# Block-sorted attention and a squared-ReLU layer: x^T of one head pair by TensorE, key copies by VectorE alone, one more pair of tiles by seven products, and a new order

## The chip, the cores and the metric

The kernel runs on one core of a Trainium2 chip. The metric is the device time of one execution in microseconds. The core has TensorE (PE, matmuls, with its weight loads shown apart as PEld), VectorE (DVE), ScalarE (ACT), GpSimd (POOL), SyncE (SP, which here only issues DMAs), and 16 DMA engines. Each engine works through its own instructions in the order in which the program lists them; engines wait for each other through semaphores. A difference of about 0.2% can be told from none for this kernel.

## The reference

Four batches, eight heads, 768 positions of 64 dimensions. A small matrix per head (8 x 8 blocks) is made nearly doubly stochastic by five rounds of exponential and normalisation; it mixes the blocks of 96 positions of the keys and of the values; each block of queries attends to its own mixed block. The result, as 3072 tokens of 512 values, goes through two matrix products with a squared ReLU between them.

```python
for _ in range(5):
    P = np.exp(P - np.max(P, axis=-1, keepdims=True))
    P = P / (np.sum(P, axis=-1, keepdims=True) + 1e-09)
    P = P / (np.sum(P, axis=-2, keepdims=True) + 1e-09)
k_sorted = np.einsum('bhij,bhjcd->bhicd', P, k_b)      # and v_sorted
attn = softmax(scale * q_b @ k_sb^T);  x = attn @ v_sb  # per block of 96
h = np.maximum(x @ w_in, 0.0)                           # 512 -> 2048
out = h * h @ w_out                                     # 2048 -> 512
```

(The softmax is written short here; in the reference it is spelled out.)

## The kernel before

**Attention.** A unit is one batch b (0 to 3, called batches 1 to 4) and one pair of heads hp (0 to 3), in stages that the program names by letters. For batch 1 and half of batch 2, keys and values are mixed by large matmuls with expanded matrices (K, V, L659 and L695). For the rest, `s_nat` (N for the keys, V for the values; L815) mixes them in their natural layout with 32 x 32 matmuls, evacuates them to `kn` and `vn` (ACT and DVE, one bank each), and the transposition is left to the DMA: `s_turn` (Z) issues a DMA transpose of `kn` into `kx` (k_turn, L870) and one of the queries, `qi` into `qz` (q_turn, L897); k_blocks then copies `kx` (128 x 768) into the tile `kvT`, in the order of positions that the scores want. The values go to a DRAM scratch `v_way` and come back as `vblk` (L839, L845). Then follow the scores (S: L730 on PE, the exponential into `et` on ACT, L759), the product with the values (A: L921, then a reciprocal and a multiplication on DVE, L931 and L932, which write `ao`), and x^T (X, `s_xt`): `ao` is transposed into the tile `xT`, either by a DMA transpose that SP issues (L956) or by TensorE (L974) with a copy out of PSUM by ACT or DVE.

**The layer.** `up_block` multiplies w_in by x^T (L1066), ACT takes the ReLU into `h` (L1074), and ACT or DVE squares it into `hid` (L1081, L1083). `plain_block` multiplies one tile of 128 tokens by w_out: 16 matmuls of 512 columns (L1153) and a copy out. `pair_block` multiplies two tiles of 128 tokens at once by a two-by-two block scheme with seven products instead of eight: sums of `hid` on DVE (L1201, written into a part of `xT` that is free), seven products of 8 matmuls of 256 columns each (L1241, with w_out or the precomputed sums `wsum`), kept parts (copied out by ACT or DVE into `xT`) and joins on DVE (L1272, which add a kept part to a product and write `ob`, 128 x 256). The products are called p1a, p2a, p1b, p2b, p5, p6, p3, p7, p4; p4 goes to the bank that p7's join frees. Batch 1 has two groups of 384 tokens with three plain blocks each, the other batches have groups of 256 tokens with one pair block each, the last one with its end taken apart.

**What sets the order.** The program first lists every operation with a cost and its dependencies, in a planner (`Plan`). DUES gives each attention stage a due time, which sorts the stages and says how much of the layer's matmul work has to pass before a stage may be preferred to it. LEAD says how many pieces of the next up block come ahead of the last block of a group, LAG how many places the last product (p4) is moved back among them. The planner then plays the program through with its costs: an operation that allows ACT or DVE (AD) goes to the one that would end it first. The order in which it starts the operations is the order of the program, for every engine. So a changed cost or due time can move any instruction.

**DMA gates.** The loads of batches 3 and 4 (`kb`, `vb`, `qb`, issued by POOL) are held back by `load_late`: a copy of a few elements of `xT` on POOL (hold) waits for the DMA transposes of x^T of the batch before. A similar copy (gate) early in the program orders one transpose behind a load. The first key of `s_turn`'s DMA transposes waits until all loads of its batch are there.

Of the kernel before, what the change touches and what calls it, by code (L numbers as in the profile page):

```python
# [18 lines left out]


DUES = {
    (0, "K"): (-816.984375, -817.0, -816.96875, -709.984375),
    (0, "S"): (-718.96875, -816.953125, -718.984375, -709.96875),
    (0, "T"): (-760.5, -816.9375, -719.0, -709.953125),
    (0, "A"): (-718.0, -734.5, -718.953125, -623.984375),
    (0, "X"): (-710.0, -624.0, -718.5, -599.0),
    (0, "W"): (-719.0,),
    (1, "V"): (-625.5, -599.0),
    (1, "Q"): (-599.0,),
    (1, "N"): (None, -598.984375),  # L30
    (1, "Z"): (None, None, -598.96875, -598.953125),
    (1, "S"): (-599.0, 33.5, 38.015625, 47.5),
    (1, "A"): (38.0, 36.5, 40.5, 47.5),
    (1, "X"): (47.53125, 40.5, 47.515625, 47.5),
    (2, "L"): (55.0,),
    (2, "N"): (69.515625, 62.5),
    (2, "V"): (69.5, 69.5625),
    (2, "Z"): (69.53125, 69.546875, 69.578125, 83.515625),
    (2, "S"): (69.59375, 89.0, 89.015625, 89.03125),
    (2, "A"): (83.5, 89.0, 89.078125, 89.046875),  # L40
    (2, "X"): (83.53125, 89.0625, 92.515625, 92.5),
    (3, "L"): (125.5,),
    (3, "N"): (125.53125, 125.515625),
    (3, "V"): (125.5, 134.5),
    (3, "Z"): (134.546875, 129.5, 134.515625, 136.015625),
    (3, "S"): (136.0, 134.5, 134.5625, 136.046875),
    (3, "A"): (136.0, 134.53125, 136.0, 136.0625),
    (3, "X"): (171.5, 136.03125, 138.5, 161.5),
}

TURNED = 1
WSUM = 0
LEAD = (0, 0, 2, 8, 0, 2, 12, 0, 12, 14, 1)
LAG = (0, 0, 2, 1, 2, 1, 2, 0, 2, 2, 0)


FIRST = ("K0' v0 K1 v1 S0 t0' S1 t1' A0 K2' V2 A1 K3 S2 t2 v3 S3 x1' A2 T3' x0' A3 X2' F0 F1 F3 "
# [155 lines left out]
def kernel(  # L215
# [213 lines left out]
    def loads_after(deps):  # L429
        for g in range(4):  # L430
            if g == 1:
                landed["last"] = plan.add("DMA", 0.4, lambda e: None, [landed["last"]])
            t = slice(NT // 4 * g, NT // 4 * (g + 1))
            dma(("w_out", g), 1.05, lambda t=t: (w_out_bf[:, t, :], w_out_r[:, t, :]), deps)
        def gate(e):
            nc.gpsimd.tensor_copy(out=xT[0:1, 0:HP - 1, HS:HS + 1],
                                  in_=w_out_bf[0:1, NT // 2 - HP + 1:NT // 2, 0:1])

        for t, g in ((2, 0), (2, 1), (1, 0), (0, 0), (1, 1), (0, 1)):
            if t == 0 and g == 1:  # L440
                holds["gate"] = plan.add("POOL", 0.1, gate, [landed["w_out", 1]])
                deps = [holds["gate"]]
            load(1, t, HP * g, HP, deps=deps)
            if t == 2 and g == 1:
                landed["last"] = plan.add("DMA", 1.5, lambda e: None, [landed["last"]])
# [417 lines left out]
    def s_turn(u):  # L863

        b, hp = u.b, u.hp
        m, op = k_nat[b, hp]
        kx, oldx = rkx.take()

        def k_turn(e):
            nc.sync.dma_start_transpose(  # L870
                out=kx_r[kx].rearrange("p (a x) -> p a x", a=NA),
                in_=kn_r[m].rearrange("p a e d -> p (a e d)"))

        def k_blocks(e):
            copy(e, u.ksT[:, 0:S].rearrange("p (n x) -> p n x", n=NB),
                 kx_r[kx].rearrange("p (x n) -> p n x", n=NB))

        sp = plan.add("SP", 1.4, k_turn, [op, loaded(b)] + oldx)
        k_op = plan.add("WAY", 1.3, lambda e: None, [sp])
        rkn.use(m, k_op)  # L880
        u.k_op = plan.add(AD, (0.8, 0.87), k_blocks, [k_op] + u.old)
        rkx.use(kx, k_op, u.k_op)

        n, oldi = rqi.take()

        def q_pair(e):
            nc.vector.tensor_copy(
                out=qi_r[n].rearrange("p a e d -> p e a d"),
                in_=qkv[b][0][:, 2 * hp:2 * hp + 2, :].rearrange("p e (a d) -> p e a d", d=D))

        qp = plan.add("DVE", 0.4, q_pair, [landed[b, 0, HP * (2 * hp // HP), 0]] + oldi)
        readers[b].append(qp)
        rqi.use(n, qp)
        u.qz, oldz = rqz.take()

        def q_turn(e):
            nc.sync.dma_start_transpose(  # L897
                out=q_late(u.qz), in_=qi_r[n].rearrange("p a e d -> p (a e d)"))

        sp = plan.add("SP", 1.4, q_turn, [qp, loaded(b)] + oldz + [op for ops in rvs.all for op in ops])  # L900
        u.q_op = plan.add("WAY", 1.3, lambda e: None, [sp])
        rqi.use(n, u.q_op)
        rqz.use(u.qz, u.q_op)

    def s_av(u, due=0):
        nao, olda = rao.take()
        if u.b > 0:
            w, u.vs_op = v_blk[u.b, u.hp // 2]
        u.norms = []
        for hf in u.halves:  # L910
            st = {}

            slot, old = r2.take()

            def mm(e, hf=hf, st=st, slot=slot):
                if hf == u.halves[0]:
                    u.ao = att.tile([96, u.ni, 2, D], BF16, tag="ao", name="ao", bufs=3)
                st["p"] = oup = p2[slot]
                for n in range(NQ):
                    for h in range(2):  # L920
                        nc.tensor.matmul(  # L921
                            out=oup[:, h, 66 * n:66 * n + D + 1],
                            lhsT=et_r[u.et[hf]][:, h, BLK * n:BLK * n + 128],
                            rhs=(u.vs[:, NQ * hf + n, h, 0:D + 1] if u.b < 1 else
                                 vb_r[w][:, NQ * hf + n, 2 * (u.hp % 2) + h, 0:D + 1]),
                            start=True, stop=True)

            def norm(e, st=st, n0=NQ * hf - u.i0):
                ov = st["p"][0:96, :, 0:66 * NQ].rearrange("p e (n x) -> p e n x", x=66)
                rec = att.tile([96, 2, NQ], FP32, tag="rec", name="rec")  # L930
                nc.vector.reciprocal(out=rec, in_=ov[:, :, :, D])  # L931
                nc.vector.tensor_tensor(  # L932
                    out=u.ao[:, n0:n0 + NQ, :, :].rearrange("p n e d -> p e n d"),
                    in0=ov[:, :, :, 0:D],
                    in1=rec[:, :, :, None].to_broadcast([96, 2, NQ, D]),
                    op=ALU.mult)

            s2 = slot
            pe = plan.add("PE", 0.26, mm, u.exps[hf] + [u.vs_op] + old
                          + (olda if hf == u.halves[0] else []), due)  # L940
            op = plan.add("DVE", 0.9, norm, [pe])
            r2.use(s2, pe, op)
            ret.use(u.et[hf], pe)
            if u.b < 1:
                rvs.use(u.m, pe)
            else:
                rvb.use(w, pe)
            u.norms.append(op)
        u.nao = nao

    def s_xt(u, due=0, eng=AD, own=True):
        early = u.b == 0 and u.halves == (1,) and u.hp < TURNED
        if early or u.b > 1 or u.b == 1 and u.hp < HP - 1:
            def turn(e):
                t0 = S * u.b + BLK * u.i0
                nc.sync.dma_start_transpose(  # L956
# [96 lines left out]
    def up_block(t0, n, c0, g):  # L1053
# [7 lines left out]
        def one(nts):  # L1061
# [23 lines left out]
            def add(m):  # L1085
# [12 lines left out]
                if m < len(nts) - 1:  # L1098
# [1 line left out]
                w = n * len(nts)  # L1100
                s1, old1 = rh1.take()
                r = plan.add("ACT", cost_f(w)[0], relu, st["pe"] + old1)
                sq = plan.add(AD, cost_b(w), square,
                              [r] + [u for c in chunks for u in h_users[c][-1:]])
                rf.use(st["s"], r)
                rf.pinned.discard(st["s"])
# [232 lines left out]
    def ffn_all():  # L1339
        ups = [up_block(0, HS, 0, 0), up_block(HS, HS, 1, 1)]  # L1340
        pairs = [[plain_block(0, 0) + plain_block(TT, 1) + plain_block(2 * TT, 2)],
                 [plain_block(HS, 1) + plain_block(HS + TT, 2) + plain_block(HS + 2 * TT, 3)]]
        for t0 in range(S, n_tok, 2 * TT):
            g = len(ups)
            c = 2 * (g % 2)
# [3 lines left out]
        for g, up in enumerate(ups):  # L1349
            items += up  # L1350
            after = ups[g + 1] if g + 1 < len(ups) else []
            for n, block in enumerate(pairs[g]):
                if n == len(pairs[g]) - 1:
                    items += after[:LEAD[g]]
                    del after[:LEAD[g]]
                items += block
                if g > 1:
                    moves.append((block[-1], LAG[g] if n == len(pairs[g]) - 1 else 1))
            if g == 0:
                items.append(weight_sums)  # L1360
# [81 lines left out]
    def load_late(b, n, due):  # L1442

        def hold(e):
            nc.gpsimd.tensor_copy(out=held[0:1, 0:HP - (b == 2), b:b + 1],  # L1445
                                  in_=xT[0:1, 0:HP - (b == 2), S * b - 1:S * b])

        holds[b] = plan.add("POOL", 0.1, hold, [x_done[b - 1, x, 0] for x in range(HP - (b == 2))])
        landed["last"] = plan.add("DMA", 4.5, lambda e: None, [holds[b]])
        for g in range(2):  # L1450
            for t in (1, 2, 0):
                load(b, t, HP * g, HP)
# [52 lines left out]
```

## Time and profile before

| | |
|---|---|
| median of 3 runs | 215.31 us (215.30 to 215.32) |
| profiled execution | 215.62 us, of which the span from first to last instruction 213.8 us |
| mean granted TensorE clock | 0.999 of full |
| PE busy | 205.9 us, 2435 matmuls |
| ACT busy | 138.6 us, 272 instructions |
| DVE busy | 136.6 us, 355 instructions |
| POOL busy | 28.2 us |
| DMA | 31.77 MB, mean 149 GB/s |

How to read it: a row of groups names the line, the engine, the operation, what it writes and reads with shapes, and how often; then the busy time in us and the mean in ns of one, and the idle time of the engine ahead of them with what ended it. The chain is the work that ended last, followed back from the end of the program: each piece stands with its start, its length, and its engine and line. A window's row gives its bounds, its length, and the busy time of PE, PEld, DVE, ACT and POOL with the number of instructions, then the clock granted to PE, the DMA engines' share and GB/s. The profile gives matmul ends that are modelled, so a busy PE is not one at its peak.

### The profile page before, as it was taken

What the parts mean: (1) busy time and instruction counts of PE and PEld (TensorE: products, weight loads), DVE (VectorE), ACT (ScalarE), POOL (GpSimd) and SP (SyncE); (2) the same over time, 40 slices, a digit from 0 to 9 for tenths busy, and PEclk for the clock granted to TensorE, in tenths of its full rate; (3) what the DMA queues carried; (4) which work ended last, traced back from release to release, by engine and by line L of the source; (5) the groups of instructions that cost most, each with busy time, mean ns of one, the idle gap of its engine ahead of it and who ended that gap; (6) DMA issues with size and microseconds to landing.
All of it is one profiled execution on the core that took longest, in us unless ns stands there. A gap on an engine that the chain in (4) does not pass through costs nothing.

```text
span 213.8 us, 5958 instructions
## 1 busy us (share of the span) xinstructions
PE 205.9 (96%) x2435; PEld 154.7 (72%) x2435; DVE 136.6 (64%) x355; ACT 138.6 (65%) x272; POOL 28.2 (13%) x54
## 2 busy tenths in 40 slices
PE   8998999999999999999999899999999999999994
PEld 2566765445654588687878688877988788888882
DVE  5877769644584427867966637677869647436442
ACT  4787997339993456579889256388769268538230
POOL 7769221000000700000000420000000000000000
PEclk9999999999999999999999999999999999999999
DMA  6999999999684799299984499759995510020022
GB/s 150 216 202 206 207 207 209 191 231 286 139 187 63 137 213 227 61 186 209 188 141 141 69 179 243 145 163 107 260 158 147 103 67 3 0 101 0 0 101 98
DMA packets 47035, 31.77 MB, mean 149 GB/s; under 512 B 26464, under 2 KB 42080, under 8 KB 47008
## 3 DMA queue, kind: packets, MB, share of 16 engines
q0 software_dynamic: 12224, 13.24, 37.8%
q1 hardware_dynamic: 34784, 18.15, 37.6%
q8 instruction: 19, 0.31, 0.6%
q14 instruction: 8, 0.07, 0.1%
HBM read 29.70 MB, written 8.72 MB: 180 GB/s over the span
## 4 chain that ended last, share of the span: by engine, by line
PE 80%; ACT 10%; DVE 5%; issue 3%; DMA 1%; DVEq 0%; ACTq 0%
PE pf L1066 33%; PE pf L1241 23%; PE pf L1153 9%; PE p L730 3%; PE p L921 3%; ACT h L1074 2%; ACT kvT L284 2%; PE p L815 2%; ACT et L759 2%; ACT hid L1081 1%; DVE xT L1201 1%; PE p L695 1%; DMA p_sb<-in_sort_net_dram 1%; PE p L486 1%; PE vbp L779 1%
## 5 line engine op out<-in xcount | busy, mean ns | idle before, releaser
L1066 PE MATMUL pf<-xT,w_in_bf 128*128 128x256 bf16 (+1 forms) x698 | 89.4, 282 | 0.1
L1066 PEld LDWEIGHTS <-w_in_bf 128*128 128x128 bf16 x698 | 66.1, 98 | 14.6 <-issue 1.4
L1074 ACT ACTIVATE h<-pf 128x512 bf16<-128x512 f32 (+1 forms) x104 | 56.9, 568 | 20.5 <-PE pf L1066 19.4
L1083 DVE TENSOR_TENSOR hid<-h 128x512 bf16<-128x512 bf16 (+1 forms) x82 | 33.1, 405 | 30.4 <-ACT h L1074 29.2
L1241 PEld LDWEIGHTS <-xT 128*128 128x128 bf16 x288 | 27.4, 98 | 5.0 <-DVE xT L1201 1.2
L1241 PE MATMUL pf<-wsum,xT 128*128 128x256 bf16 x216 | 27.1, 273 | 0.1
L1241 PEld LDWEIGHTS <-hid 128*128 128x128 bf16 x216 | 20.6, 98 | 3.5 <-issue 1.1
L932 DVE TENSOR_TENSOR ao<-p,rec 96x512 bf16<-96x512 f32 x32 | 22.0, 687 | 1.1
L1153 PE MATMUL pf<-w_out_bf,hid 128*128 128x512 bf16 x96 | 22.6, 379 | 0.0
L284 ACT COPY xT<-pf 128x256 f32<-128x256 f32 (+1 forms) x28 | 10.6, 377 | 18.2 <-PE pf L1241 12.2
L759 ACT ACTIVATE et<-p 96x384 bf16<-96x384 f32 x48 | 19.7, 492 | 2.4 <-PE p L730 2.4
L284 ACT COPY ob<-pf 128x256 f32<-128x256 f32 (+1 forms) x14 | 6.5, 464 | 19.9 <-PE pf L1153 12.3
L1272 DVE TENSOR_TENSOR ob<-pf,xT 128x256 f32<-128x256 f32 x27 | 11.4, 424 | 11.0 <-PE pf L1241 8.7
L1241 PE MATMUL pf<-w_out_bf,hid 128*128 128x256 bf16 x144 | 18.0, 273 | 0.0
L1153 PEld LDWEIGHTS <-hid 128*128 128x128 bf16 x96 | 8.7, 97 | 9.2 <-issue 0.2
L931 DVE RECIPROCAL rec<-p 96x8 f32<-96x8 f32 x32 | 6.4, 200 | 12.1 <-PE p L921 10.4
L921 PEld LDWEIGHTS <-et 96*128 96x128 bf16 x256 | 11.4, 97 | 3.5 <-issue 0.8
L1201 DVE TENSOR_TENSOR xT<-hid 128x512 bf16<-128x512 bf16 (+1 forms) x27 | 13.0, 510 | 0.6
L1081 ACT ACTIVATE hid<-h 128x512 bf16<-128x512 bf16 (+1 forms) x22 | 12.9, 593 | 0.5
L1445 POOL COPY held<-xT 1x3 bf16<-1x3 bf16 (+1 forms) x2 | 0.4, 186 | 83.1 <-DMA xT<-ao 83.1
L1241 PE MATMUL pf<-w_out_bf,xT 128*128 128x256 bf16 x72 | 9.4, 273 | 0.6 <-DVE xT L1201 0.6
L1241 PE MATMUL pf<-wsum,hid 128*128 128x256 bf16 x72 | 9.3, 272 | 0.6 <-DVE ob L1272 0.5
(103 smaller groups left out, 203.5 us busy)
## 6 DMA issues: line engine op xcount, KB each, us to landing
out_dram<-ob SPq DMA_DIRECT2D x23, 256.0 KB, 2.5
v_way<-vn SPq DMA_DIRECT2D x6, 396.0 KB, 5.7
vblk<-v_way SPq DMA_DIRECT2D x6, 396.0 KB, 4.3
vb<-in_v_dram POOLq DMA_DIRECT2D x6, 384.0 KB, 12.9
kb<-in_k_dram POOLq DMA_DIRECT2D x6, 384.0 KB, 11.6
qb<-in_q_dram POOLq DMA_DIRECT2D x6, 384.0 KB, 14.3
w_in_bf<-in_moe_w_in_dram POOLq DMA_DIRECT2D x4, 512.0 KB, 9.7
w_out_bf<-in_moe_w_out_dram POOLq DMA_DIRECT2D x4, 512.0 KB, 13.9
```

Of the source, the lines that this page charges most:

```text
L284: nc.scalar.copy(out=out, in_=in_)
L759: nc.scalar.activation(out=et[:, h, 0:HS].rearrange("p (n c a) -> p n c a", c=C0, a=NA), in_=st["p"][0:96, h, 0:HS].rearrange("p (n a c) - ...
L921: nc.tensor.matmul(out=oup[:, h, 66 * n:66 * n + D + 1], lhsT=et_r[u.et[hf]][:, h, BLK * n:BLK * n + 128], rhs=(u.vs[:, NQ * hf + n, h, 0: ...
L932: nc.vector.tensor_tensor(out=u.ao[:, n0:n0 + NQ, :, :].rearrange("p n e d -> p e n d"), in0=ov[:, :, :, 0:D], in1=rec[:, :, :, None].to_b ...
L1066: nc.tensor.matmul(out=pf_r[st["s"]][:, n * m:n * (m + 1)], lhsT=w_in_bf[:, kc, 128 * nt:128 * (nt + 1)], rhs=xT[:, kc, t0:t0 + n], start= ...
L1074: nc.scalar.activation(out=st["h1"][:, 0:n * len(nts)], in_=pf_r[st["s"]][:, 0:n * len(nts)], func=AF.Relu)
L1081: nc.scalar.activation(out=dst, in_=h1, func=AF.Square)
L1083: nc.vector.tensor_tensor(out=dst, in0=h1, in1=h1, op=ALU.mult)
L1153: nc.tensor.matmul(out=pf_r[st["s"]], lhsT=hid[:, nt, TT * c:TT * (c + 1)], rhs=w_out_bf[:, nt, :], start=(nt == 0), stop=(nt == NT - 1))
L1201: lambda e: nc.vector.tensor_tensor(out=s_view(n, js), in0=a, in1=bb, op=op), deps + st["old", n])
L1241: nc.tensor.matmul(out=pf_r[st[bank]][:, cols], lhsT=a, rhs=r, start=(first and j == 0), stop=(j == NJ - 1), skip_group_check=n in (3, 4, ...
L1272: op = plan.add("DVE", 0.15 + 1.04e-3 * DH, lambda e: nc.vector.tensor_tensor(out=get()[:, cols], in0=pf_r[st[bank]][:, 0:DH], in1=buf, op ...
```

## The change

- `s_xt`: for batches 3 and 4 (b = 2, 3), the last head pair's x^T (hp = 3) is made by eight TensorE transposes and a copy of 128 x 768 out of PSUM, where it was a DMA transpose. CROSS says for each batch how many head pairs still use the DMA. Batch 4's loads are accordingly held for three transposes, not four, and the early gate reads one column, not three.
- k_blocks may run on DVE alone; before, the planner chose between ACT and DVE.
- Batch 1's second group of 384 tokens: one plain block and one pair block instead of three plain blocks.
- All due times, LEAD and LAG are new, and three costs of the planner (q_pair, norm, the square on ACT), so that the stages and with them the instructions of every engine stand in a new order. LAG now applies to every block that ends with p4.

The first line of CROSS moves all later lines by one: L974 is L975 in the changed kernel, and so on.

```diff
 DUES = {
-    (0, "K"): (-816.984375, -817.0, -816.96875, -709.984375),
+    (0, "K"): (-924.375, -959.328125, -1014.625, -571.03125),
...
-    (3, "X"): (171.5, 136.03125, 138.5, 161.5),
+    (3, "X"): (173.046875, 152.640625, 167.296875, 157.984375),
 }
+CROSS = (0, 3, 3, 3)
 TURNED = 1
 WSUM = 0
-LEAD = (0, 0, 2, 8, 0, 2, 12, 0, 12, 14, 1)
-LAG = (0, 0, 2, 1, 2, 1, 2, 0, 2, 2, 0)
+LEAD = (0, 0, 2, 12, 0, 10, 8, 0, 12, 14, 14)
+LAG = (3, 3, 2, 3, 3, 1, 3, 0, 2, 2, 3)
...
         def gate(e):
-            nc.gpsimd.tensor_copy(out=xT[0:1, 0:HP - 1, HS:HS + 1],
-                                  in_=w_out_bf[0:1, NT // 2 - HP + 1:NT // 2, 0:1])
+            nc.gpsimd.tensor_copy(out=xT[0:1, 0:TURNED, HS:HS + 1],
+                                  in_=w_out_bf[0:1, NT // 2 - TURNED:NT // 2, 0:1])
...
-        u.k_op = plan.add(AD, (0.8, 0.87), k_blocks, [k_op] + u.old)
+        u.k_op = plan.add("DVE", 0.87, k_blocks, [k_op] + u.old)
...
-        qp = plan.add("DVE", 0.4, q_pair, [landed[b, 0, HP * (2 * hp // HP), 0]] + oldi)
+        qp = plan.add("DVE", 0.36, q_pair, [landed[b, 0, HP * (2 * hp // HP), 0]] + oldi)
...
-            op = plan.add("DVE", 0.9, norm, [pe])
+            op = plan.add("DVE", 0.92, norm, [pe])
...
-        if early or u.b > 1 or u.b == 1 and u.hp < HP - 1:
+        if early or u.b > 0 and u.hp < CROSS[u.b]:
...
-                sq = plan.add(AD, cost_b(w), square,
+                sq = plan.add(AD, (cost_b(w)[0] + 0.04, cost_b(w)[1]), square,
...
-                 [plain_block(HS, 1) + plain_block(HS + TT, 2) + plain_block(HS + 2 * TT, 3)]]
+                 [plain_block(HS + 2 * TT, 3), pair_block(HS, HS + TT, 1, 2, 0)]]
...
-                if g > 1:
+                if block[-1].__name__ == "p4":
                     moves.append((block[-1], LAG[g] if n == len(pairs[g]) - 1 else 1))
...
-            nc.gpsimd.tensor_copy(out=held[0:1, 0:HP - (b == 2), b:b + 1],
-                                  in_=xT[0:1, 0:HP - (b == 2), S * b - 1:S * b])
+            nc.gpsimd.tensor_copy(out=held[0:1, 0:CROSS[b - 1], b:b + 1],
+                                  in_=xT[0:1, 0:CROSS[b - 1], S * b - 1:S * b])
 
-        holds[b] = plan.add("POOL", 0.1, hold, [x_done[b - 1, x, 0] for x in range(HP - (b == 2))])
+        holds[b] = plan.add("POOL", 0.1, hold, [x_done[b - 1, x, 0] for x in range(CROSS[b - 1])])
```

How the instructions stand at three places, before and in the change. In the rows, `kvT_92`, `kx_130`, `kn_125`, `qi_126`, `et_131`, `wsum_161`, `vblk_121` and the like are buffers of the tiles named above, `p_0_78`, `p_1_79` and `pf_80` to `pf_82` are PSUM banks, and `xtp` is the PSUM tile of the TensorE transposes.

ACT before, at batch 3's last head pair: two kept parts of a pair block, the key copy for the last scores, and the exponentials of the third and the fourth head pair.

```order
L284 COPY xT<-pf_82 128x256
L284 COPY xT<-pf_81 128x256
L284 COPY kvT_92<-kx_130 128x768
L759 ACTIVATE et_131<-p_0_78 96x384 x2
L759 ACTIVATE et_134<-p_1_79 96x384 x2
L759 ACTIVATE et_137<-p_0_78 96x384 x2
L284 COPY ob<-pf_81 128x256
```

DVE in the change, where the same copy now stands:

```order
L287 COPY kvT_108<-kx_129 128x768
L932 RECIPROCAL rec<-p_0_78 96x8
L933 TENSOR_TENSOR ao<-p_0_78,rec 96x2x4x64
L932 RECIPROCAL rec<-p_1_79 96x8
L933 TENSOR_TENSOR ao<-p_1_79,rec 96x2x4x64
L287 COPY kvT_92<-kx_130 128x768
L1273 TENSOR_TENSOR ob<-pf_81,xT 128x256
L1273 TENSOR_TENSOR ob<-pf_82,xT 128x256
```

The copy left ACT's queue, where exponentials were behind it, for DVE's, where two joins are behind it.

PE before, in the pair block that runs beside the end of batch 4's attention, from p7 (`wsum_161`) to p4 (`wsum_162`):

```order
L1241 MATMUL pf_82<-wsum_161,xT 128x256
L1241 LDWEIGHTS xT
L1241 MATMUL pf_82<-wsum_161,xT 128x256
L1241 LDWEIGHTS hid
L1241 MATMUL pf_82<-wsum_162,hid 128x256
```

And in the change:

```order
L1242 LDWEIGHTS xT
L1242 MATMUL pf_82<-wsum_161,xT 128x256
L975 LDWEIGHTS ao
L975 MATMUL xtp<-ident,ao 128x96
L975 LDWEIGHTS ao
L975 MATMUL xtp<-ident,ao 128x96
L975 LDWEIGHTS ao
```

Eight transposes (the first are shown) now stand between the two products.

SP before, at the end of batch 4's transposes:

```order
L870 DMA_TRANSPOSE kx_130<-kn_125 128x6x128
L897 DMA_TRANSPOSE qz_97<-qi_126 128x6x128
L845 DMA vblk_121<-v_way 96x2112
L956 DMA_TRANSPOSE xT<-ao 128x8x96
L1127 DMA out_dram<-ob 128x512 x2
L956 DMA_TRANSPOSE xT<-ao 128x8x96 x3
```

And in the change:

```order
L871 DMA_TRANSPOSE kx_130<-kn_125 128x6x128
L898 DMA_TRANSPOSE qz_97<-qi_126 128x6x128
L957 DMA_TRANSPOSE xT<-ao 128x8x96
L846 DMA vblk_121<-v_way 96x2112
L1128 DMA out_dram<-ob 128x512 x3
L957 DMA_TRANSPOSE xT<-ao 128x8x96 x2
```

The first x^T transpose moved ahead of the read of the values, and the fourth one is gone.

More of the change, by code (lines that the diff above doesn't have):

```diff
@@ L21 @@
 DUES = {
-    (0, "K"): (-816.984375, -817.0, -816.96875, -709.984375),
[L23 to L45, printed above, removed]
@@ L46 @@
-    (3, "S"): (136.0, 134.5, 134.5625, 136.046875),
-    (3, "A"): (136.0, 134.53125, 136.0, 136.0625),
-    (3, "X"): (171.5, 136.03125, 138.5, 161.5),
+    (0, "K"): (-924.375, -959.328125, -1014.625, -571.03125),
+    (0, "S"): (-915.09375, -924.8125, -910.28125, -482.65625),
+    (0, "T"): (-576.4375, -926.625, -883.203125, -570.125),
+    (0, "A"): (-563.34375, -892.640625, -856.546875, -424.234375),
+    (0, "X"): (-415.0, -878.71875, -417.515625, -421.5),
+    (0, "W"): (-894.859375,),
+    (1, "V"): (-418.078125, -417.4375),
@@ new lines @@
+    (1, "Q"): (-416.0625,),
+    (1, "N"): (None, -415.9375),
+    (1, "Z"): (None, None, 30.03125, 35.0625),
+    (1, "S"): (33.5, 35.9375, 36.0625, 38.03125),
+    (1, "A"): (36.03125, 36.046875, 37.953125, 38.046875),
+    (1, "X"): (38.015625, 40.921875, 40.9375, 42.953125),
+    (2, "L"): (41.5,),
+    (2, "N"): (43.25, 60.203125),
+    (2, "V"): (63.734375, 81.46875),
+    (2, "Z"): (68.296875, 70.84375, 90.734375, 91.03125),
+    (2, "S"): (81.46875, 90.890625, 91.0, 91.140625),
+    (2, "A"): (85.46875, 90.96875, 91.015625, 91.46875),
@@ L49 @@
+    (2, "X"): (90.296875, 100.046875, 91.84375, 97.28125),
+    (3, "L"): (104.28125,),
+    (3, "N"): (115.921875, 112.328125),
+    (3, "V"): (120.859375, 123.515625),
+    (3, "Z"): (135.3125, 123.0, 123.5, 140.5),
+    (3, "S"): (147.0, 123.90625, 145.09375, 154.15625),
+    (3, "A"): (149.28125, 127.078125, 152.609375, 155.5),
+    (3, "X"): (173.046875, 152.640625, 167.296875, 157.984375),
 }
+CROSS = (0, 3, 3, 3)
 TURNED = 1
 WSUM = 0
-LEAD = (0, 0, 2, 8, 0, 2, 12, 0, 12, 14, 1)
-LAG = (0, 0, 2, 1, 2, 1, 2, 0, 2, 2, 0)
+LEAD = (0, 0, 2, 12, 0, 10, 8, 0, 12, 14, 14)
```

## The prediction

> **What bounds the kernel now.** I read the page's busy shares first, then the chain, then the windows at the places where TensorE (PE) stands idle, then the groups by form.
>
> ```profile
> PE 205.9 (96%) x2435; PEld 154.7 (72%) x2435; DVE 136.6 (64%) x355; ACT 138.6 (65%) x272; POOL 28.2 (13%) x54
> ...
> PE 80%; ACT 10%; DVE 5%; issue 3%; DMA 1%; DVEq 0%; ACTq 0%
> ```
>
> PE is busy for 96% and makes up 80% of the chain that ended last. So there are only two ways to gain: fewer matmul microseconds, or less idle time of PE. The next view gives the idle time (window, its length, PE busy, then weight loads, DVE, ACT and POOL).
>
> ```profile
> 12.00:171.00 159.00, 155.53 (x1944) 114.77 (x1945) 107.25 (x238) 109.72 (x214) 19.91 (x38) 1.00 0.91 173
> 18.00:20.00 2.00, 1.50 (x25) 1.21 (x23) 1.81 (x6) 1.33 (x3) 2.00 (x3) 1.00 1.25 210
> 61.00:65.00 4.00, 3.70 (x46) 2.07 (x45) 3.31 (x7) 4.00 (x12) 0.00 (x0) 1.00 0.85 143
> 98.00:99.00 1.00, 0.58 (x11) 0.29 (x10) 0.09 (x1) 1.00 (x2) 0.00 (x0) 1.00 1.65 279
> 119.00:122.00 3.00, 2.30 (x20) 1.55 (x18) 1.77 (x4) 1.12 (x3) 1.68 (x4) 1.00 0.30 47
> 149.00:150.00 1.00, 0.73 (x19) 0.64 (x20) 0.40 (x2) 1.00 (x3) 0.00 (x0) 1.00 0.57 203
> 169.00:171.00 2.00, 1.49 (x15) 1.18 (x13) 0.76 (x2) 0.00 (x0) 0.00 (x0) 1.00 0.72 170
> ```
>
> From 12 to 171 us PE idles 159.00 - 155.53 = 3.47 us, of which 0.50, 0.30, 0.42, 0.70, 0.27 and 0.51 lie in the six short windows, 2.70 together. That pool is about all that a better order can win. What ended the waits is in the chain (start, length, what):
>
> ```profile
> 97.25 1.59 ACT kvT L284
> 98.89 0.51 PE p L730 x16
> ...
> 108.32 1.16 ACT kvT L284
> ...
> 118.20 1.04 DVE xT L1201 x2
> ...
> 147.61 1.61 ACT kvT L284
> 149.27 0.51 PE p L730 x16
> ...
> 169.71 0.43 DVE ob L1272
> 170.19 1.03 PE pf L1241 x8
> ```
>
> At 98.89 and 149.27 the scores (L730) wait for ScalarE's (ACT's) copy of the sorted keys into kvT. At 108.32 such a copy delays the exponentials behind it on ACT, these the squares, these the sums on VectorE (DVE, L1201), and after 119 the products that read the sums pay. At 170.19 p4 waits for the join of p7, which stands right ahead of it.
>
> **The copies into kvT.**
>
> ```profile
> L284 ACT COPY kvT<-kx 128x768 bf16<-128x768 bf16 x5 | 8.0, 1591 | 0.0
> L286 DVE COPY kvT<-kx 128x768 bf16<-128x768 bf16 x5 | 4.2, 850 | 0.0
> ```
>
> ACT takes 1.59 us, DVE 0.85, and of ten such copies each had five. All ten are now DVE's: ACT loses 8.0 us of 138.6, DVE gains 4.2. Engine totals cost or win nothing by themselves (both were at 65%); what counts is where the copy stands. The one of 108.32 stood on ACT right ahead of the exponentials of batch 3's last head pair, and on DVE it now stands between a norm and two joins (first pieces of the order, above). The exponentials no longer have it ahead of them; the joins behind it come later by 0.85, and a matmul block waits for the bank that each frees. I count the windows at 98 (0.42), 119 (0.70) and 149 (0.27) as gone: -1.39. With two of them goes a slow restart, since the scores take 0.51 there and 0.45 in a place without a wait (below): -0.1. If DVE comes late to the copies or the joins, this returns; that is a rival.
>
> **Matmul work.** Batch 1's second half had three plain blocks; two of them become one pair block of seven products.
>
> ```profile
> 50.68 0.45 PE p L730 x16
> ...
> 64.95 0.87 PE pf L1153 x4
> ...
> 74.04 0.34 PE xtp L974 x8
> ...
> 123.37 0.87 PE pf L1066 x8
> ```
>
> Two plain blocks are 32 matmuls of 512 columns, 0.87/4 each: -6.96. The seven products are 56 matmuls of 256 columns, 0.87/8 each (L1066 has the same shape): +6.09. The two x^T blocks of the last head pair add 16 transposes at 0.34/8: +0.68. The sum is -0.19: most of what the seven products save goes into the transposes. The pair block also adds six sums and three joins on DVE and some copies on ACT; the blocks around it are another 7 us of matmuls and more, with no evacuation of a plain block to wait for, so I price them at nothing, and at 0.4 (one join, as at 169.71) if p4 should wait there.
>
> The Trainium skill, "TensorE: Matmul & The Clock Gate", Part 4 (PE-mode transpose), speaks against the transposes: it gives about 275 ns for one of 128x128 bf16 in a kernel's context, so 16 would be an estimated 4.4 us and the change would lose. The row above has eight in 0.34 us, 43 ns apiece; the trace differs, and the sum keeps 0.68.
>
> **x^T of the last head pair.** Before, a DMA transpose followed the last norm; now PE and a copy do it.
>
> ```profile
> L286 DVE COPY xT<-xtp 128x768 bf16<-128x768 bf16 x1 | 0.6, 558 | 1.1 <-PE xtp L974 1.1
> xT<-ao SPq DMA_TRANSPOSE x12, 3.2
> ```
>
> 3.2 us from issue to landing become 0.34 on PE and 0.56 on DVE, so x^T is ready 2.3 us sooner. The up block that reads it did not wait for it at 171 before (p4 ran until then), so this counts only in that it lets the block follow sooner. In batch 4 the transposes stand between p7 and p4 (second pieces). Before, p4's first row came right behind p7's last. The eight transposes, 0.34 us, cover most of the 0.51 that PE idled for p7's join: -0.3.
>
> **The rest of the order.** The windows at 18 (0.50) and 61 (0.30) keep dependencies of the same kind (an exponential or a copy on ACT ahead of an L921); the bounds are all or nothing, I take half: -0.4. The four joins of batch 4's keys and values come closer to each other, with 0.9 us of other matmuls between two of them, while an evacuation takes up to 0.96:
>
> ```profile
> L286 DVE CAST vn<-p 128x768 bf16<-128x768 f32 x6 | 5.7, 956 | 1.8 <-PE p L815 1.7
> L931 DVE RECIPROCAL rec<-p 96x8 f32<-96x8 f32 x32 | 6.4, 200 | 12.1 <-PE p L921 10.4 <-ACT h L1074 1.5
> L932 DVE TENSOR_TENSOR ao<-p,rec 96x512 bf16<-96x512 f32 x32 | 22.0, 687 | 1.1
> ```
>
> Three such gaps could each cost up to 0.2, so 0 to 0.6, and I take +0.3.
>
> **What SP gets to wait for.** Ahead of the last read of batch 4's values (vblk) there now stands an x^T, which waits for ao; before, vblk came first (third pieces). SP's rows of before:
>
> ```profile
> 142.07 1.24 SPq L870 DMA_TRANSPOSE kx<-kn  x1
> 144.74 2.11 SPq L870 DMA_TRANSPOSE kx<-kn  x1
> 148.01 1.92 SPq L897 DMA_TRANSPOSE qz<-qi  x1
> 154.39 1.24 SPq L897 DMA_TRANSPOSE qz<-qi  x1
> 155.72 0.53 SPq L845 DMA_DIRECT2D vblk<-v_way  x1
> 156.35 1.95 SPq L956 DMA_TRANSPOSE xT<-ao  x1
> vblk<-v_way SPq DMA_DIRECT2D x6, 396.0 KB, 4.3
> ```
>
> In the new order 64 matmuls of 0.109 (7.0 us), two score steps (0.9) and two half steps of L921 (0.5) lie between the L921 that feeds this ao and the first that reads vblk: 8.4 us. The way there: two norms of 0.20 + 0.69 (1.8), the issue of the transpose (1.24 to 1.95), that of vblk (0.53) and 4.3 to landing, 7.9 to 8.6 if SP is free. SP's pace: from the first kx at 142.07 to the end of the last qz at 155.63 it took 13.6 us; in the new order 14.4 us of blocks lie between batch 4's first join (L815) and that L921; the first kx goes out 4 us after that join, behind a v_way that waits for the third one's evacuation, and the norms add 1.8, so it has 12.2 us, and by that pace SP is 1.4 us late. But part of the pace was a wait for ACT's copies to free kx, which now take half as long. PE waits 0 to 1.8 us; I take +0.5, and +0.1 at batch 3, where x^T also stands ahead of a vblk. Queued behind on PE is everything, since it works in order.
>
> **The sum**, from the profiled execution (215.62 us: span 213.8 and 1.8 around it; 0.31 above the median of 215.31): -1.39 - 0.1 - 0.19 - 0.3 - 0.4 + 0.3 + 0.5 + 0.1 = -1.48. That is 214.1 for a profiled execution and **213.8 us** for the median. With the open bounds, the likeliest case lies between 212.8 and 214.8.
>
> **Rivals.**
>
> *DVE becomes the bound of the last attention stage.* Copies, joins, sums and norms go through one queue in order:
>
> ```profile
> L1201 DVE TENSOR_TENSOR xT<-hid 128x512 bf16<-128x512 bf16 (+1 forms) x27 | 13.0, 510 | 0.6
> ```
>
> In the new order six norms (5.3 us), four sums (2.0), three joins and a copy of the output (1.7) and one square (0.4) stand in a row, 9.4 us, beside 10.3 us of PE's blocks: hardly any slack, and a norm that waits for its L921 holds all behind it. Against it: the rows overlap a little, and norms before were done in time. Then the 1.5 us come back as waits for ao and joins: 215.3, no change.
>
> *SP's queue makes vblk late by much* (the slower side). The mechanism is that above. If all eight transposes of batch 4 issue at 1.95 us instead of 1.24 (+5.7 us), vblk lands some 4 us after its need instead of 0.5, and batch 3's 1 us late: 213.8 + 3.5 + 0.9 = 218.2 at the most, and 216.2 halfway to it. From 1.5 us more lateness than I took, it outweighs the gain. For it: two of the rows above were at 1.92 and 2.11. Against: the others were at 1.24.
>
> *The gain is not on the path.* Other waits of the same length stand behind those removed, on ACT above all, whose relus and exponentials still set when banks come free. Only the matmul sum is left: 215.1, no change.
>
> *The transposes don't overlap each other.*
>
> ```profile
> L974 PE MATMUL xtp<-ident,ao 96*128 96x96 bf16 x24 | 1.9, 206 | 0.0
> ```
>
> One by one they would take 16 x 0.206 = 3.3 us instead of 0.68: 213.8 + 2.6 = 216.4. By the skill's page above it would be an estimated 217.5. The row of eight in 0.34 us leaves it a chance of 0.01.
>
> **How the numbers follow.** Forecast 0.62, DVE bound 0.14, SP late 0.11, no gain 0.12, transposes 0.01. About 0.2% (0.43 us) is what a measurement of this kernel can tell from no change, so faster is below 214.88. Nearly all of the forecast falls there (0.60), and of the DVE, SP and no-gain cases those parts in which only some waits return (0.11): faster 0.71. Slower: 0.09 of SP's, 0.05 of DVE's and 0.01: 0.15. The rest, 0.14, is no change. The range 212.3 to 215.9 leaves out one in ten on either side: below it all six windows would be gone with nothing new in their place; above it SP is late by more than 2 us.
>
> **What would show it.** Right: PE idle between 12 and 171 us at some 2.3 us; no L730 behind a kvT copy of 1.59; ACT's busy time near 132 and DVE's near 146; ten DMA transposes of x^T instead of twelve. Wrong: idle time before L921 released by the landing of vblk, or before L730 and L974 by DVE's ao. PE's idle time as before with 0.2 less busy time would be the third rival. The forecast fails if one place has a stall over 1.5 us, or if the start, whose order is new throughout, loses more than 0.5.

## The result and the profile after

The changed kernel takes **213.9 us** (median) against 215.35 for the kernel before on the same chip, a ratio of 0.9937 with an interval of 0.9918 to 0.9957. It is faster by 1.45 us. A second set of runs gave 213.85 against 215.42, 0.993 (0.9912 to 0.9949). The forecast was 213.8.

The page of the changed kernel, its head:

```profile
span 212.3 us, 6031 instructions
...
PE 204.6 (96%) x2472; PEld 157.6 (74%) x2475; DVE 144.4 (68%) x369; ACT 133.5 (63%) x271; POOL 28.2 (13%) x54
```

The span fell by 1.5 us. ACT lost 5.1 us, DVE gained 7.8. PE's busy time seems to fall by 1.3 (205.9 to 204.6), but three matmuls have no record here (2472 against 2475 weight loads). The same kernel's second profile ("the changed kernel again", below) has them all:

```profile
PE 205.2 (97%) x2475; PEld 158.1 (74%) x2475; DVE 144.6 (68%) x369; ACT 133.6 (63%) x271; POOL 28.2 (13%) x54
```

By it PE's busy time fell by 0.7, and what is not busy, the span less the busy time, from 7.9 to 7.1. The same windows as before (window, length, PE, PEld, DVE, ACT, POOL, clock, DMA share, GB/s):

```profile
12.00:171.00 159.00, 155.85 (x1997) 119.14 (x2000) 115.25 (x252) 105.55 (x215) 19.82 (x38) 1.00 0.91 172
18.00:20.00 2.00, 1.50 (x26) 1.24 (x23) 1.81 (x6) 1.33 (x3) 2.00 (x3) 1.00 1.25 209
98.00:99.00 1.00, 1.00 (x12) 0.83 (x9) 1.00 (x3) 0.97 (x3) 0.00 (x0) 1.00 0.82 144
119.00:122.00 3.00, 3.00 (x31) 2.68 (x29) 1.62 (x4) 0.60 (x1) 2.72 (x5) 1.00 0.56 116
149.00:150.00 1.00, 1.00 (x21) 0.93 (x18) 0.69 (x2) 0.21 (x2) 0.00 (x0) 1.00 1.16 322
156.00:161.00 5.00, 3.18 (x48) 2.67 (x46) 2.93 (x7) 3.79 (x8) 0.00 (x0) 1.00 0.89 219
167.00:170.00 3.00, 2.83 (x32) 2.48 (x30) 1.92 (x5) 0.37 (x1) 0.00 (x0) 1.00 0.23 87
```

The waits at 98, 119 and 149 are gone, the one at 18 is unchanged, p4's fell from 0.51 to 0.17, and between 156 and 161 there is a new one of 1.82. PE's timeline names it (start, length, what, and in brackets the idle time before it and its releaser):

```profile
18.96 0.41 PE L922 MATMUL p<-qz,et 96*128 96x65 bf16 x8 [0.50 <-ACT qz L285]
...
160.74 0.67 PE L922 MATMUL p<-vblk,et 96*128 96x65 bf16 x16 [1.82 <-DMA vblk<-v_way]
168.55 1.03 PE L1242 MATMUL pf<-wsum,hid 128*128 128x256 bf16 x8 [0.17 <-DVE ob L1273]
```

So the one wait that the prediction named as the price of the change is there, and it is more than half of all the idle time that is left between 12 and 171 us (3.15 us; in the second profile 1.74 of 2.80). SP's rows and DVE's norm show why:

```profile
147.46 2.76 SPq L871 DMA_TRANSPOSE kx<-kn  x1
150.28 1.29 SPq L898 DMA_TRANSPOSE qz<-qi  x1
151.63 0.69 DVE L933 TENSOR_TENSOR ao<-p,rec 96x512 bf16<-96x512 f32 x1
151.66 1.77 SPq L871 DMA_TRANSPOSE kx<-kn  x1
153.53 1.24 SPq L898 DMA_TRANSPOSE qz<-qi  x1
154.86 1.24 SPq L957 DMA_TRANSPOSE xT<-ao  x1
156.19 0.53 SPq L846 DMA_DIRECT2D vblk<-v_way  x1
```

The ao that the x^T transpose waits for was ready at 152.3. The transpose went out at 154.86, right behind the last qz. So it did not hold the queue by its wait: the queue was late by its own pace, and the transpose added its 1.24 us of issue ahead of vblk.

### The profile page after: what moved, and what is told of

It is laid out like the page before. It is cut to its first block, busy times and chain, and to the rows that moved or that the text cites. A ratio compares the mean times of both kernels' runs of the same rounds, so it can differ in the third digit from the quotient of the medians.

```text
span 212.3 us, 6031 instructions
## 1 busy us (share of the span) xinstructions
PE 204.6 (96%) x2472; PEld 157.6 (74%) x2475; DVE 144.4 (68%) x369; ACT 133.5 (63%) x271; POOL 28.2 (13%) x54
## 5 line engine op out<-in xcount | busy, mean ns | idle before, releaser
L1075 ACT ACTIVATE h<-pf 128x512 bf16<-128x512 f32 (+1 forms) x104 | 58.0, 570 | 23.8 <-PE pf L1067 22.6
L1084 DVE TENSOR_TENSOR hid<-h 128x512 bf16<-128x512 bf16 (+1 forms) x77 | 31.3, 407 | 29.5 <-ACT h L1075 28.8
L1242 PEld LDWEIGHTS <-xT 128*128 128x128 bf16 x320 | 30.4, 98 | 4.1 <-issue 0.5
L1242 PE MATMUL pf<-wsum,xT 128*128 128x256 bf16 x240 | 30.5, 273 | 0.0
L1242 PEld LDWEIGHTS <-hid 128*128 128x128 bf16 x240 | 22.8, 98 | 3.6 <-issue 0.7
L285 ACT COPY xT<-pf 128x256 f32<-128x256 f32 (+1 forms) x30 | 11.3, 377 | 19.4 <-PE pf L1242 12.8
L1242 PE MATMUL pf<-w_out_bf,hid 128*128 128x256 bf16 x160 | 20.4, 273 | 0.0
L1202 DVE TENSOR_TENSOR xT<-hid 128x512 bf16<-128x512 bf16 (+1 forms) x30 | 14.8, 510 | 2.2 <-ACT xT L285 1.4
L1082 ACT ACTIVATE hid<-h 128x512 bf16<-128x512 bf16 (+1 forms) x27 | 15.8, 594 | 0.7
L1154 PE MATMUL pf<-w_out_bf,hid 128*128 128x512 bf16 x61 | 14.6, 379 | 0.3 <-issue 0.2
L922 PEld LDWEIGHTS <-et 96*128 96x128 bf16 x256 | 11.0, 97 | 4.6 <-DMA vblk<-v_way 2.1
L922 PE MATMUL p<-vblk,et 96*128 96x65 bf16 x192 | 9.1, 193 | 1.8 <-DMA vblk<-v_way 1.8
```

The lines of the kernel that those rows point to most:

```text
L285: nc.scalar.copy(out=out, in_=in_)
L922: nc.tensor.matmul(out=oup[:, h, 66 * n:66 * n + D + 1], lhsT=et_r[u.et[hf]][:, h, BLK * n:BLK * n + 128], rhs=(u.vs[:, NQ * hf + n, h, 0: ...
L1075: nc.scalar.activation(out=st["h1"][:, 0:n * len(nts)], in_=pf_r[st["s"]][:, 0:n * len(nts)], func=AF.Relu)
L1082: nc.scalar.activation(out=dst, in_=h1, func=AF.Square)
L1084: nc.vector.tensor_tensor(out=dst, in0=h1, in1=h1, op=ALU.mult)
L1154: nc.tensor.matmul(out=pf_r[st["s"]], lhsT=hid[:, nt, TT * c:TT * (c + 1)], rhs=w_out_bf[:, nt, :], start=(nt == 0), stop=(nt == NT - 1))
```

## The experiments

The kernels are named by what they change. Moves in the order are made in the list of operations that the planner hands out, after it has run, so that nothing else moves; where the planner had to run again, it is said. The times of one group share a chip and the runs of the kernel before. Where an edit adds lines, the lines behind it have higher numbers: by one in "before, with three squares on DVE", by seven in "x^T of batch 4 by DMA, in place".

**vblk ahead of x^T**: one SP instruction put ahead of another.

```diff
-    for op in plan.run():
+    order = plan.run()
+    at = {getattr(op, "tag", None): op for op in order}
+    order.remove(at["vblk", 3, 1])
+    order.insert(order.index(at["xT", 3, 1]), at["vblk", 3, 1])
+    for op in order:
```

> The changed kernel with two instructions of SP exchanged: the read of batch 4's last values (vblk) goes ahead of the x^T transpose that it stood behind; nothing else moves. Theory A (SP's queue makes vblk late, and PE's L922 waits 1.8 us for it): vblk issues 1.33 us sooner (at 154.9 where it was 156.2), the wait falls to about 0.5, and the time from 213.9 to 212.6. Rival B (PE would wait for something else at that place anyway, a norm on DVE or the exponentials): the wait changes its releaser and the time stays at 213.9.

Measured: 212.87 us against 215.58, ratio 0.9871 (0.9845 to 0.9898).

**vblk ahead of qz**: the same with the last qz in the place of x^T.

```diff
+    order.insert(order.index(at["qz", 3, 3]), at["vblk", 3, 1])
```

> The changed kernel with the same read moved two places ahead on SP: before the last query transpose (qz) too. Theory A: vblk issues at about 153.5, 2.7 us sooner, the wait of 1.8 is gone, time 212.1; the last qz goes 0.6 later and still lands ahead of its scores. Rival B: 213.9. Rival C (the delayed qz is then what PE waits for): the wait moves to the last scores, 212.5 to 213.0.

Measured: 212.49 against 215.58, ratio 0.9861 (0.9838 to 0.9884). And a second time, as the base for later ones:

> The changed kernel with the read of batch 4's last values two places ahead on SP, a second time, as the base for the next two: 212.0 to 212.8, as before.

Measured: 212.45 against 215.55, ratio 0.9856 (0.9841 to 0.987). SP's rows of the first of the three:

```profile
147.88 1.79 SPq L871 DMA_TRANSPOSE kx<-kn  x1
...
152.99 1.24 SPq L898 DMA_TRANSPOSE qz<-qi  x1
154.32 0.53 SPq L846 DMA_DIRECT2D vblk<-v_way  x1
```

PE's waits after the start, in the second run of "vblk ahead of qz":

```profile
18.91 0.41 PE L922 MATMUL p<-qz,et 96*128 96x65 bf16 x8 [0.50 <-ACT qz L285]
43.52 4.26 PE L1154 MATMUL pf<-w_out_bf,hid 128*128 128x512 bf16 x19 [0.16 <-issue]
166.88 1.03 PE L1242 MATMUL pf<-wsum,hid 128*128 128x256 bf16 x8 [0.17 <-DVE ob L1273]
```

No L922 waits for vblk any more, and nothing took its place: theory A holds, rivals B and C fall. In its profiled execution the first exchange brought vblk forward by 1.87 us instead of the 1.33 that were expected, since a kx transpose that had taken 2.76 us took 1.79; its six runs spread from 211.95 to 213.85. The intervals of the two exchanges overlap, so their times do not tell them apart. With the second, a span of 212.3 became 210.6. This is the version that beats both kernels, by 1.4% against the one before.

**Four copies on ACT**: in the changed order, four key copies go back to ACT.

```diff
+    for x in (("kvT", 2, 0), ("kvT", 2, 3), ("kvT", 3, 0), ("kvT", 3, 3)):
+        at[x].eng = "ACT"
```

> The changed kernel with the four key copies of batches 3 and 4 that ACT did in the kernel before (first and last head pair of each) back on ACT, at the place in the order where DVE had them. Theory A (a copy of 1.59 us on ACT ahead of scores and exponentials is what cost the windows at 98, 119 and 149): 0.8 to 1.4 us more, 214.7 to 215.3. Rival D (the new places of the stages made the difference, the engine does not matter, since the copies now come well ahead of the scores): 213.9 within 0.3; if DVE was the tight engine, even 213.6.

Measured: 215.87 against 215.58, ratio 1.0011 (1.0001 to 1.0022). That is 1.6 to 1.7 us more than the changed kernel by the ratios (0.9937 and 0.993): theory A's side, and above its 0.8 to 1.4. PE's waits:

```profile
99.75 0.51 PE L731 MATMUL p<-qz,kvT 64*128 64x96 bf16 x16 [0.58 <-ACT kvT L285]
103.22 0.93 PE L1242 MATMUL pf<-w_out_bf,hid 128*128 128x256 bf16 x7 [0.23 <-ACT h L1075]
156.53 0.35 PE L731 MATMUL p<-qz,kvT 64*128 64x96 bf16 x8 [0.83 <-ACT et L760]
157.29 0.34 PE L731 MATMUL p<-qz,kvT 64*128 64x96 bf16 x8 [0.41 <-ACT et L760]
160.76 0.41 PE L922 MATMUL p<-vblk,et 96*128 96x65 bf16 x8 [1.02 <-ACT et L760]
```

One wait is for the copy itself, 0.58, and one for a ReLU, 0.23. The others are for exponentials behind a copy on ACT, 2.26 together. The last of them lies where the changed kernel waits for vblk, and vblk came no earlier here (issued at 156.43, 4.4 us to landing), so that wait has two causes; the waits of this list are 1.25 us more than the changed kernel's 1.82 for vblk. The same copies were not tried with vblk moved ahead.

**Before, with its copies on DVE**: the reverse in the kernel before.

```diff
+    for x in [("kvT", b, hp) for b in (1, 2, 3) for hp in range(4) if ("kvT", b, hp) in at]:
+        at[x].eng = "DVE"
```

> The kernel before with all its key copies on DVE, at the same places in the order; nothing else is changed. Theory A: the windows at 98 (0.42), 119 (0.70) and 149 (0.27) lose their waits, 1.0 to 1.4 us less: 214.0 to 214.3 against 215.35. Rival D (the order, not the engine, made the gain; joins and norms behind the copies on DVE come later by 0.85): 215.0 to 215.6.

Measured: 215.79 against 215.58, ratio 1.0009 (0.9997 to 1.0021): no gain. PE's waits after the start:

```profile
60.86 0.41 PE L921 MATMUL p<-vblk,et 96*128 96x65 bf16 x8 [0.61 <-DVE ao L932]
111.59 1.03 PE L1241 MATMUL pf<-wsum,hid 128*128 128x256 bf16 x8 [0.37 <-DVE ob L1272]
121.79 1.05 PE L1241 MATMUL pf<-w_out_bf,xT 128*128 128x256 bf16 x8 [0.63 <-DVE xT L1201]
164.21 0.35 PE L730 MATMUL p<-qz,kvT 64*128 64x96 bf16 x8 [0.44 <-DVE ao L932]
170.54 1.03 PE L1241 MATMUL pf<-wsum,hid 128*128 128x256 bf16 x8 [0.51 <-DVE ob L1272]
```

Both waits for kvT are gone, as theory A says, and three others of 0.61, 0.37 and 0.44 have come, all for a norm or a join that stands behind a copy on DVE. The wait at 121 is still 0.63, so the copy at 108 was not its cause. Theory A falls for the kernel before: the engine alone wins nothing there. With the run above, the rest of the change (the new order, the pair block, the transposes) wins nothing either with four of the ten copies on ACT. The gain needs both.

**Before, with three squares on DVE**: what makes the wait at 121?

```diff
+    first = order.index(at["kvT", 2, 3])
+    for op in [op for op in order[first:] if getattr(op, "tag", " ")[0] == "sq" and op.eng == "ACT"][:3]:
+        op.eng = "DVE"
```

> The kernel before, with the three squares that ACT makes at 114 to 117 on DVE, at the same places; nothing else. With the key copies on DVE the wait of 0.63 at 121.5 had stayed. Theory S (that wait comes from ACT doing a relu and a square in turn, 0.60 + 0.63, for four tiles, which is slower than the up steps on PE; the copy at 108 is not its cause): the wait shrinks to under 0.3, and the time by 0.3 to 0.6 us. Rival T (the sums on DVE behind the squares are the limit, or norms come later): the wait stays and the time is the same within 0.2.

Measured: 215.65 against 215.55, ratio 1.0011 (1.0001 to 1.0021). The wait stays at 0.55, and a new one of 0.40 for a square on DVE comes ahead of it:

```profile
117.98 1.26 PE L1242 MATMUL pf<-w_out_bf,hid 128*128 128x256 bf16 x10 [0.40 <-DVE hid L1083]
121.54 1.05 PE L1242 MATMUL pf<-w_out_bf,xT 128*128 128x256 bf16 x8 [0.55 <-DVE xT L1202]
```

What theory S forecast did not come, as rival T said; since a square came late on DVE instead, the run does not show what shorter work on ACT alone would do. In the timeline of the kernel before, what runs up to that wait is DVE's own row: the last square, the sums, a sum that waits for ACT's kept part, a join, and the sum that p3 reads:

```profile
118.20 1.03 DVE L1201 TENSOR_TENSOR xT<-hid 128x512 bf16<-128x512 bf16 x2
119.31 0.76 ACT L284 COPY xT<-pf 128x256 f32<-128x256 f32 x2 [1.61 <-DVE xT L1201]
119.72 0.43 DVE L1201 TENSOR_TENSOR xT<-xT,hid 128x512 bf16<-128x512 bf16 x1 [0.49 <-ACT xT L284]
120.24 0.43 DVE L1272 TENSOR_TENSOR ob<-pf,xT 128x256 f32<-128x256 f32 x1
120.70 0.69 DVE L1201 TENSOR_TENSOR xT<-hid,xT 128x1024 bf16<-128x1024 bf16 x1
```

PE had only products between the last up step and p3. In the changed order two halves of L731 and two of L922 stand among the products of this block, ahead of p3, and there the wait is zero. That this is what removed it is read from the two orders and was not tried by itself.

**x^T by DMA, planned anew**, on top of "vblk ahead of qz".

```diff
-CROSS = (0, 3, 3, 3)
+CROSS = (0, 3, 4, 4)
```

> The base with x^T of the last head pair by DMA again in batches 3 and 4 (the planner sets the order anew around it). Theory G (the 16 transposes cost 0.68 us of PE, and save 0.3 of the wait of p4 plus whatever the up block would wait for the DMA): between 0.4 faster and 0.2 slower than the base; the wait ahead of p4 grows from 0.17 to about 0.5. Rival H (the DMA's 3.2 us to landing are on the path at the end of the batch): a wait of the up block L1067 for the x^T transpose of 1 us or more, 0.5 to 2 us slower.

Measured: 218.82 against 215.55, ratio 1.0147 (1.0119 to 1.0176), 2.9% above its base. PE's waits:

```profile
121.36 1.14 PE L1067 MATMUL pf<-xT,w_in_bf 128*128 128x256 bf16 x9 [1.23 <-DMA xT<-ao]
...
172.74 13.46 PE L1067 MATMUL pf<-xT,w_in_bf 128*128 128x256 bf16 x109 [2.32 <-DMA xT<-ao]
```

Rival H holds, and more: these two waits are 3.55 us of some 6.3. The planner had moved other work too: three more waits of 0.42, 0.42 and 0.37, for ACT and DVE, stand between 161 and 170 us. And part of the loss is the clock, which was 1.00 in the base:

```profile
171.00:185.00 14.00, 12.26 (x100) 10.46 (x100) 6.55 (x15) 7.85 (x14) 0.00 (x0) 0.88 0.13 34
```

At 0.88 these 12.26 us of matmuls are an estimated 1.5 us longer; five of the six runs had a mean clock of 0.992, and the one at 1.00 took 217.41. What lowered the clock is not shown. So it was repeated for batch 4 alone, in place.

**x^T of batch 4 by DMA, in place.**

```diff
+        by_dma = u.b == 3
         def ev(e):
             t0 = S * u.b + BLK * u.i0
+            if by_dma:
+                nc.sync.dma_start_transpose(
+                    out=xT[:, u.hp, t0:t0 + BLK * u.ni].rearrange("p (n q) -> p n q", q=BLK),
+                    in_=u.ao.rearrange("p n e d -> p (n e d)"))
+                return
...
-        pe = plan.add("PE", 0.342 if u.full else 0.17, mm, u.norms + old, due)
+        pe = plan.add("PE", 0.342 if u.full else 0.17, (lambda e: None) if by_dma else mm, u.norms + old, due)
```

> The kernel with vblk two places ahead, where batch 4's last x^T is a DMA transpose again, issued right behind its last norm, and the eight TensorE transposes and the copy are left out; every other instruction keeps its place (when the planner had set the order anew, the waits of the up blocks for the DMA were 1.2 and 2.3 us). Theory H (the DMA's way of about 3 us is on the path in this order, since only p7, p4 and little else stand behind the norm): the up block waits 1.0 to 2.3 us for it, and p4 0.5 instead of 0.17; 1.0 to 2.3 us slower than 212.45: 213.5 to 214.8. Rival G (those waits came from the order set anew): within 0.3 of 212.45, or 0.3 faster by the transposes' time.

Measured: 213.37 against 215.42, ratio 0.9901 (0.9884 to 0.9918), where the base has 0.9856: about 0.9 us slower, just under the expected range.

```profile
167.08 1.03 PE L1249 MATMUL pf<-wsum,hid 128*128 128x256 bf16 x8 [0.52 <-DVE ob L1280]
169.18 12.06 PE L1074 MATMUL pf<-xT,w_in_bf 128*128 128x256 bf16 x109 [0.73 <-DMA xT<-ao]
```

p4's wait is 0.52 instead of 0.17, and the up block waits 0.73 for the DMA. Less the 0.34 of the transposes that makes 0.74, of 0.9 measured; a wait of 0.23 for a key copy on DVE at 155.27, ahead of the edit, is in this execution too. So in batch 4 alone TensorE's transposes are worth about 0.9 us in this order, give or take 0.5 by the two intervals.

**The changed kernel again**, for the same chip as the last and the next:

> The changed kernel itself, a second time, so that the others of this group are compared with it on one chip: 213.9 as before, with the wait of 1.8 us for vblk.

Measured: 213.85 against 215.42, with the wait for vblk at 1.74:

```profile
160.80 0.67 PE L922 MATMUL p<-vblk,et 96*128 96x65 bf16 x16 [1.74 <-DMA vblk<-v_way]
```

**Batch 1 in plain blocks**, planned anew, on top of "vblk ahead of qz".

```diff
-                 [plain_block(HS + 2 * TT, 3), pair_block(HS, HS + TT, 1, 2, 0)]]
+                 [plain_block(HS, 1) + plain_block(HS + TT, 2) + plain_block(HS + 2 * TT, 3)]]
...
-                if block[-1].__name__ == "p4":
+                if g > 1:
```

> The base with batch 1's second group as three plain blocks again (the planner then sets the order anew). Theory E (the pair block saves its matmul difference, 6.96 - 6.09 = 0.87 us, and DVE's sums and joins are hidden): 0.87 us slower than the base, plus or minus 0.3, and no new wait of PE in batch 1. Rival F (the extra sums, joins and kept copies cost as much in waits as the products save): the same as the base within 0.3.

Measured: 220.53 against 215.55, ratio 1.0215 (1.018 to 1.0249), 8 us above its base. Neither theory foresaw that. PE's largest waits lie in the later batches:

```profile
113.65 0.66 PE L922 MATMUL p<-vblk,et 96*128 96x65 bf16 x16 [0.79 <-DMA vblk<-v_way]
...
158.36 0.35 PE L731 MATMUL p<-qz,kvT 64*128 64x96 bf16 x8 [0.72 <-DMA qz<-qi]
161.84 0.41 PE L922 MATMUL p<-vblk,et 96*128 96x65 bf16 x8 [0.84 <-DVE ao L933]
```

The due times are counted in matmul work of the layer, and with other blocks in batch 1 they set another order everywhere behind. The run says nothing on E against F; what the pair block is worth by itself stays open.

**vblk, and one copy of the start on DVE.**

```diff
+    for x in (("vt", 0, 3, (0,)),):
+        at[x].eng = "DVE"
```

> The kernel with vblk two places ahead, and one copy of values (qz) at 18.3 us on DVE instead of ACT, the last wait over 0.2 us that is left after the start. Theory: the wait of 0.50 at 18.9 falls to about 0.2, 0.1 to 0.3 us less than 212.45. Rival: DVE's norms of the start come 0.4 later and x^T with them: the same, or 0.3 slower.

Measured: 213.08 against 215.42, ratio 0.9891 (0.9877 to 0.9906), slower than its base (0.9856). The wait doubled:

```profile
19.45 0.41 PE L922 MATMUL p<-qz,et 96*128 96x65 bf16 x8 [1.01 <-DVE qz L287]
```

DVE was the busier engine there (1.81 of the 2 us in the window, ACT 1.33), so the copy came later still, and batch 3 has a new wait of 0.46 further on. This is the rival's side, at some 0.7 us slower instead of its 0.3.

## Why the prediction was right, point by point

The time was right to 0.1 us by luck in part: two errors of about 1 us cancelled.

*Copies into kvT, -1.39 - 0.1.* The three windows did lose their waits, but the working had one cause for all three. For the windows at 98 and 149 it was the copy: the kernel before without copies on ACT has no wait there. (At 149 the term was short: the window cut off half of a wait of 0.44.) For the one at 119 (0.70, half of the term) it was not: neither the copies nor the squares on DVE took it away. And "what counts is where the copy stands" was sharper than it was used: in the old order the copies on DVE gave back 0.61, 0.37 and 0.44 as waits for norms and joins, which is the rival on DVE at work. In the new order DVE was busy 7.8 us more, and after the start PE's only wait for it of over 0.15 is at p4, 0.17; that rival did not come.

*Matmul work, -0.19.* Consistent with the trace, not shown apart. PE's busy time, its head in "vblk ahead of qz" and its first 20 us before and in that run:

```profile
PE 205.0 (97%) x2475; PEld 158.1 (75%) x2475; DVE 144.4 (69%) x369; ACT 133.6 (63%) x271; POOL 28.2 (13%) x54
...
0.00:20.00 20.00, 17.83 (x323) 10.62 (x324) 15.62 (x88) 14.40 (x30) 15.67 (x32) 1.00 1.10 193
0.00:20.00 20.00, 18.03 (x323) 10.82 (x324) 15.53 (x88) 14.32 (x30) 15.66 (x32) 1.00 1.11 194
```

The second profile of that kernel has 204.2, with three matmuls unrecorded and 17.37 in the first 20 us, so the whole sum differs by 0.8 between executions of one kernel. Behind the first 20 us, and with every matmul on record, PE's busy time fell from 188.1 to 187.2 in the changed kernel and to 187.0 in "vblk ahead of qz". If the matmul sum holds, 0.7 to 0.9 us of the busy time before belonged to the waits (argued from the sums, no run shows it by itself). One reason fits: a matmul of 256 columns has a record of 273 ns, while in a row each takes 0.109 us, so up to 0.16 us of a wait lies under the record of the matmul ahead of it; four waits fewer make up to 0.65, an estimate. The pool of 3.47 us that the prediction read from the windows was too small: it holds only the time in which no matmul stood on PE at all, and the term for slow restarts, -0.1, should have been seven to nine times as large.

*x^T of the last head pair.* p4's wait: -0.3 forecast, 0.51 to 0.17 measured, and with the DMA in place 0.52 again: right, with its cause. That the up block did not wait for the DMA transpose held for the old order alone, where it came late enough. In the new order it waits 0.73 in batch 4, and 1.23 and 2.32 when the planner sets the order around it. In batch 4 the new order needs the transposes; batch 3's were not tried by themselves. The row of eight in 0.34 us stood against the 275 ns that the Trainium skill, "TensorE: Matmul & The Clock Gate", Part 4 (PE-mode transpose), gives for one of 128x128; the 0.9 us gained by them in batch 4 alone leaves no room for eight times that, an estimated 2.2 us.

*The rest of the order.* Half of the windows at 18 and 61 was taken. The one at 18 stayed whole (0.50), the one at 61 went almost whole (0.30 to 0.05): the sum is near, the halves are wrong. The +0.3 for crowded joins (L816) did not come; PE has no wait there.

*SP's queue, +0.5 + 0.1.* Place and releaser were right, and of the two ways that were priced it was SP's pace and not the path through the norms, whose ao was ready 2.5 us before its transpose went out. The size was not right: 1.82 and 1.74 us, the upper end of the bounds that were given (0 to 1.8). The step that failed was the credit for the copies that free kx sooner: SP did not get faster. From the first kx at 139.62 to the end of the last qz at 154.77 it took 15.2 us, against the 13.6 of before; 1.2 of the 1.6 more are longer issues (14.0 us in all against 12.8). Why they took longer stays open.

```profile
139.62 2.07 SPq L871 DMA_TRANSPOSE kx<-kn  x1
```

Batch 3's 0.1 did not come. The two exchanges on SP show that the 1.8 us were all this queue's.

In sum: with the SP terms out, the forecast gain was 2.1 us; measured without that wait it is 3.1 (215.55 to 212.45). About 1.0 us too little gain (the +0.3 that did not come and the slow restarts) and some 1.2 too little SP wait made the number right. In the list of what would show it, ten transposes, ACT near 132 and DVE near 146 came true (ten, 133.5, 144.4); the idle time of "some 2.3" was 3.15 (2.80 in the second profile), through vblk. Two of the prediction's own signs of being wrong came too: idle time before L921 (now L922) released by the landing of vblk, and one place with a stall over 1.5 us. The time came out right all the same, because the gain elsewhere was larger than the prediction had said.

## What to carry to other kernels

When an instruction moves from one engine's queue to another's, list what stands behind it in both: here the same move won nothing in one order and was worth 1.6 to 1.7 us in another. Check the costs of a planner against the trace: the kernel before priced this copy at 0.8 us on ACT and 0.87 on DVE, where the rows have 1.59 and 0.85. What that planner would do with the measured cost was not tried. In a queue of DMA issues that takes over a microsecond for each transpose, put the transfer that has the next reader ahead of one whose reader is far, even when the other is ready; one exchange was worth as much as the whole change. And do not take the idle time of a pipelined engine for the whole price of its waits: by the sums above, its busy time holds some of it.

## What the runs showed of the hardware

A DMA transpose held SP for 1.24 to 2.76 us in the rows shown, and a plain read behind two of them, which went out at 153.47 when it stood ahead of them ("vblk ahead of qz"), went out at 156.19. The key copy of 128 x 768 took 1.60 us on ACT and 0.86 on DVE in the same kernel ("four copies on ACT"):

```profile
L287 DVE COPY kvT<-kx x6: 846/855/860, 56.4 to 147.2; 128x768 bf16<-128x768 bf16 x6
L285 ACT COPY kvT<-kx x4: 1549/1595/1605, 98.1 to 158.3; 128x768 bf16<-128x768 bf16 x4
```

And PE's busy time is not its work: it fell by 0.9 us from the kernel before to the best one (205.9 to 205.0, every matmul recorded), where the matmuls' own sum is 0.2 less. Two executions of that best kernel differ by almost as much (205.0 and 204.2), so a difference of this size needs more than one trace.
